# A tail tile's fifth channel block as three matmuls of 512 columns in place of six of 256

## The chip, the cores and the metric

The kernel runs on one core of one Trainium2 chip. The metric is the device time of one execution in microseconds, as the median of several runs. Engines are written as in the profile: PE for TensorE, PEld for its weight loads, DVE for VectorE, ACT for ScalarE, POOL for GpSimd, SP for SyncE, which issues most of the transfers.

## The reference, cut to what matters

The input `x` holds 2 x 4096 tokens of 640 channels in fp32. Two branches are mixed by a gate for each token: a spectral branch (a real Fourier transform over the tokens, a small block-wise network on the frequencies, and the transform back), and a gated feed-forward branch. The change lies in the second.

```python
def _B_ref(x, w_gate, w_up, w_down):
    return (_gelu(x @ w_gate) * (x @ w_up)) @ w_down      # 640 -> 1728 -> 640

x = A_x
g = _sigmoid((x * gate_w).sum(-1, keepdims=True))
a = _A_ref(x, A_w1, A_b1, A_w2, A_b2)                     # the spectral branch
b = _B_ref(x, B_w_gate, B_w_up, B_w_down)
return g * a + (1 - g) * b
```

## The kernel before

Every fp32 operand of a matmul is split into a high and a low part (`split`, lines 275 to 284: ACT copies the high part, DVE subtracts to get the low one), both kept in the type float32r. One product of two such operands is three matmuls: high by high, high by low, low by high. `prod` (line 461) writes out these three for each pair of operands, and `run` (line 470) issues the list into one part of a PSUM bank; `first` says whether the first matmul of the list starts a new sum or adds to what the bank holds.

The kernel has three stages in time. The gate and up products x @ w_gate and x @ w_up come first, up to about 1388 us, with the forward transform threaded in between (`a_step`, line 605); then the block-wise network on the frequencies; and from about 1812 us on the down product with the inverse transform. The order is written out by hand: no scheduler moves anything. `hook(k)` calls inside the products run small pieces of preparation that a table (`slots`) puts at chosen places.

In the first stage the tokens are taken in 16 blocks of 512, and the 1728 hidden columns in 14 tiles: tiles 0 to 12 have 128 gate columns and 128 up columns each, and the last, tile 13 (`NPAIR`), has the 64 gate columns and 64 up columns that remain, side by side in one weight tile of 128 columns. The tiles are dealt with in three groups (0 to 3, 4 to 7, 8 to 13); `keys` lists the pairs of group and token block, 48 in all. Tiles 0 to 12 go through `quad` (line 492), which forms the gate and up products by a scheme with seven block products of 6 or 9 matmuls each (`plain`, line 547, does the first ones directly). Tile 13 goes through `mixed` (line 564), once for each of the 16 keys of the third group, after the second `quad` of the key (line 1339). The page puts all matmuls of `run` on line 472, those of the spectral stages on line 295 (`mms`) and others.

The 640 channels are five slices of 128. Slices 0 to 3 lie in four operand tiles of 512 columns, `b11`, `b21`, `b12` and `b22`: `b11` and `b21` hold two channel slices each for the first 256 tokens of the block, `b12` and `b22` for the other 256. The fifth slice lies in `k4`, whose 512 columns are all 512 tokens of the block for that one slice. `x_of` (line 480) cuts these tiles into operands of 256 columns; `("k4", q)` asks for the q-th half of `k4`. Each is a pair of high and low. So `mixed` of before runs, for each half of the tokens, five channel slices of three matmuls each, all of 256 columns: 30 matmuls into one bank, 256 columns of it for each half.

Behind the products, `mixed` takes a gelu of the first 64 partitions (ACT, line 573), copies the other 64 (ACT, line 574), multiplies the two (DVE, line 575) and hands the result to the store `h_store`. A `memset` on POOL (line 572) clears the half of `h` that the tail tile does not fill.

Of the kernel before, what the change touches and what calls it, by code (L numbers as in the profile page):

```python
# [213 lines left out]
def spectral_mix_kernel(ctx: ExitStack, tc: tile.TileContext, a):  # L214
# [12 lines left out]
    def bank():  # L227
        return psum.tile([P, 512], F32, name="bank", tag="bank")
# [13 lines left out]
    def small(shape, dt=F32, name="small"):  # L242
        return pool.tile(shape, dt, name=name, tag="small", bufs=18)
# [217 lines left out]
    def prod(ws, x):  # L461

        ops = []
        for (wh, wl), (xh, xl) in zip(ws, x):
            ops += [(wh, xh), (wh, xl), (wl, xh)]
        return ops
# [3 lines left out]
    def run(dst, ops, first=True):  # L470
        for i, (l, r) in enumerate(ops):
            nc.tensor.matmul(dst, l, r, start=first and i == 0, stop=i == len(ops) - 1, skip_group_check=True)  # L472
            while inner and i == 1:
                inner.pop()()

    def h_store(tp, t, h):
        st(dr(hD, 4 * tp * P * 14 * P + t * P, [[14 * P, P], [P * 14 * P, 4], [1, P]]),
           h.rearrange("p (t n) -> p t n", t=4))

    def x_of(o, *names):  # L480

        tiles = []
        for n in names:
            n, q = n if isinstance(n, tuple) else (n, None)
            h, l = o[n]
            for k in ((0,) if n == "t5" else (0, 1) if q is None else (q,)):
                tiles.append((h[:, 256 * k:256 * k + 256], l[:, 256 * k:256 * k + 256]))
        return tiles
# [75 lines left out]
    def mixed(key):  # L564

        o, w = XO[key], WG[NPAIR]
        ws = [(w[:, k, 0], w[:, k, 1]) for k in range(5)]
        pm = bank()
        for q, (x0, x1) in enumerate((("b11", "b21"), ("b12", "b22"))):
            run(pm[:, 256 * q:256 * q + 256], prod(ws, x_of(o, x0, x1, ("k4", q))))  # L570
        s, h = small([P, 512], name="gelu"), small([P, 512], name="h")
        nc.gpsimd.memset(h[64:], 0.0)  # L572
        nc.scalar.activation(s[:64], pm[:64], AF.Gelu_apprx_tanh)
        nc.scalar.activation(h[:64], pm[64:], AF.Copy)
        nc.vector.tensor_mul(h[:64], s[:64], h[:64])
        h_store(key[1], NPAIR, h)
# [739 lines left out]
    for i, key in enumerate(keys):  # L1316
# [16 lines left out]
        for j, t in enumerate(quads):  # L1333
            def hook(k):
                for f in slots.get((i, 7 * j + k), ()):
                    f()
            (quad if i else plain)(key, t, hook)
            if gr == 2 and j == 1:
                mixed(key)
            if i % 16 == 15:  # L1340
                WG.pop(t)
            if 0 < i + 1 < last and j == nq - 1:
                x_raw(keys[i + 2])
            n = len(late)
            for f, *args in todo.get((i, j), []):
                f(*args)
            new = late[n:]
            del late[n:]
            flush()
            late.extend(new)  # L1350
# [126 lines left out]
```

## Time and profile before

| What | Value |
|---|---|
| Median of 3 runs | 2547.28 us |
| The three runs | 2546.24, 2550.69, 2547.28 us |
| Profiled execution | span 2546.4 us; the page lists no time of its own around it |
| Busy PE / DVE / ACT / POOL | 2535.1 / 2055.1 / 1502.8 / 370.2 us |
| Matmuls in all | 20276, of which 11736 of 256 columns from `xo` on line 472 |
| DMA | 483.48 MB, mean 190 GB/s |

The span runs from the first to the last instruction of one profiled execution. Busy times are unions: matmuls overlap, so that a PE that is busy throughout need not be at its peak, and the mean duration of one matmul in a group is its latency, not the distance to the next.

### The profile page before, as it was taken

How to read it: one execution, taken by the hardware profiler on the slowest of the kernel's cores; microseconds unless marked ns; L12 is line 12 of the kernel's file. 1: busy time of each engine (PE TensorE's matmuls, PEld its weight loads, DVE VectorE, ACT ScalarE, POOL GpSimd, SP SyncE). 2: the span in 40 equal slices, each digit the busy share in tenths (PEclk: the TensorE clock that was granted, in tenths of full speed). 3: DMA queues.
4: the chain of work that ended last, by engine and by line, in shares of the span. 5: the costliest groups of instructions: out<-in, count | busy, mean ns of one | idle time of the engine just before them, and what ended most of it. 6: DMA issues, size and time to landing. Idle time of an engine off the chain costs nothing.

```text
span 2546.4 us, 54296 instructions
## 1 busy us (share of the span) xinstructions
PE 2535.1 (100%) x20276; PEld 2530.4 (99%) x20276; DVE 2055.1 (81%) x4212; ACT 1502.8 (59%) x3490; POOL 370.2 (15%) x370
## 2 busy tenths in 40 slices
PE   9999999999999999999999999999999999999999
PEld 9999999999999999999999999999999999999999
DVE  7778777777777766776667788888899999999998
ACT  6555555666665655555556777778644444445443
POOL 0000000000000000000002111111133333333332
PEclk9999999999999999999999999999999999999999
DMA  6565657676767667776667455548844444344442
GB/s 232 190 215 196 212 170 234 205 236 211 219 205 249 207 213 231 224 230 214 212 222 223 129 153 150 160 137 266 291 149 138 150 156 158 120 144 156 155 136 92
DMA packets 346060, 483.48 MB, mean 190 GB/s; under 512 B 24701, under 2 KB 222717, under 8 KB 345797
## 3 DMA queue, kind: packets, MB, share of 16 engines
q1 hardware_dynamic: 331108, 438.47, 54.5%
q0 software_dynamic: 14688, 41.56, 4.5%
q8 instruction: 159, 2.61, 0.4%
q14 instruction: 105, 0.85, 0.1%
HBM read 300.29 MB, written 179.64 MB: 188 GB/s over the span
## 4 chain that ended last, share of the span: by engine, by line
PE 97%; DMA 1%; DVE 1%; issue 0%; ACT 0%; SPq 0%; DVEq 0%; ACTq 0%
PE bank L472 77%; PE bank L295 14%; PE bank L783 3%; PE bank L619 1%; DMA wx<-wdf 1%; PE bank L861 1%; PE bank L860 1%; DMA wx<-wdl 0%; PE bank L863 0%; DVE xo L279 0%; DMA wraw<-in_wgu_dram 0%; DVE xd L430 0%; DVE h L543 0%; DVE w L279 0%; DVE wl L715 0%
## 5 line engine op out<-in xcount | busy, mean ns | idle before, releaser
L472 PE MATMUL bank<-xo,w 128*128 128x256 f32 x11736 | 1362.0, 277 | 6.3 <-ACT xo L276 5.1
L472 PEld LDWEIGHTS bank<-xo,w 128*128 128x128 f32 x11736 | 1353.0, 188 | 7.5 <-ACT xo L276 5.1
L472 PE MATMUL bank<-wx,ho 128*128 128x320 f32 x4608 | 678.6, 308 | 0.1
L472 PEld LDWEIGHTS bank<-wx,ho 128*128 128x128 f32 x4608 | 674.1, 188 | 0.6 <-DMA wx<-wdf 0.3
L498 ACT ACTIVATE u<-bank 128x256 f32<-128x256 f32 x408 | 156.7, 384 | 258.0 <-PE bank L472 252.5
L279 DVE TENSOR_TENSOR ho<-hraw,ho 128x640 fp32r<-128x640 f32 (+3 forms) x384 | 276.9, 761 | 5.0 <-ACT ho L276 3.0
L276 ACT ACTIVATE ho<-hraw 128x640 fp32r<-128x640 f32 x320 | 166.3, 574 | 64.1 <-PE bank L472 46.8
L498 ACT ACTIVATE p<-bank 128x256 f32<-128x256 f32 x204 | 78.6, 385 | 149.0 <-PE bank L472 66.4
L279 DVE TENSOR_TENSOR xo<-xraw,xo 128x512 fp32r<-128x512 f32 x209 | 142.9, 684 | 25.2 <-ACT xo L276 24.7
L531 DVE TENSOR_TENSOR u<-bank,u 128x256 f32<-128x256 f32 x204 | 85.9, 421 | 90.8 <-ACT u L498 88.2
L279 DVE TENSOR_TENSOR xs<-xr,xs 64x640 fp32r<-64x640 f32 x128 | 105.0, 820 | 58.0 <-ACT xs L276 56.0
L1165 ACT ACTIVATE uu<-bank,gs 128x320 f32<-128x320 f32 x120 | 55.0, 525 | 160.0 <-PE bank L295 157.7
L295 PE MATMUL bank<-wm,h 128*128 128x320 f32 (+1 forms) x792 | 137.8, 309 | 0.0
L540 DVE TENSOR_TENSOR u<-bank,u 128x256 f32<-128x256 f32 x204 | 85.5, 419 | 62.2 <-PE bank L472 61.3
L276 ACT ACTIVATE xo<-xraw 128x512 fp32r<-128x512 f32 x209 | 131.0, 627 | 7.1 <-DMA xraw<-in_xT_dram 5.3
L621 DVE TENSOR_TENSOR as<-bank,as 64x320 f32<-64x320 f32 x256 | 113.9, 484 | 25.0 <-ACT as L620 24.0
L295 PEld LDWEIGHTS bank<-wm,h 128*128 128x128 f32 (+1 forms) x792 | 118.6, 185 | 1.2
L276 ACT ACTIVATE ho<-hs 128x640 fp32r<-128x640 f32 (+1 forms) x128 | 71.9, 576 | 77.8 <-PE bank L472 57.7
L572 POOL MEMSET h<- 64x512 f32 x16 | 8.4, 522 | 747.7 <-PE bank L619 369.4
L514 DVE TENSOR_TENSOR p<-bank,p 128x256 f32<-128x256 f32 x204 | 86.5, 424 | 36.6 <-PE bank L472 32.2
L279 DVE TENSOR_TENSOR s2s<-s,s2s 128x320 fp32r<-128x320 f32 x128 | 111.6, 929 | 0.9 <-ACT s2s L276 0.9
L620 ACT ACTIVATE as<-bank 64x320 f32<-64x320 f32 x256 | 96.8, 427 | 16.5 <-PE bank L619 14.0
(157 smaller groups left out, 3470.7 us busy)
## 6 DMA issues: line engine op xcount, KB each, us to landing
xo<-xD SPq DMA_DIRECT2D x124, 512.0 KB
xraw<-in_xT_dram SPq DMA_DIRECT2D x225, 256.0 KB
hD<-h SPq DMA_DIRECT2D x224, 256.0 KB
hraw<-hD SPq DMA_DIRECT2D x128, 320.0 KB
xD<-xo POOLq DMA_DIRECT2D x64, 512.0 KB, 4.4
sc<-scr SPq DMA_DIRECT2D x65, 320.0 KB
xr<-in_x_dram SPq DMA_DIRECT2D x64, 320.0 KB
scr<-as SPq DMA_DIRECT2D x64, 320.0 KB
```

The costliest lines, as they stand in the source:

```text
L276: nc.scalar.activation(dst, src, AF.Copy, scale=scale)
L279: eng.tensor_sub(dst, src, hi.bitcast(F32))
L295: nc.tensor.matmul(dst, l, r, start=i == 0, stop=i == len(ops) - 1)
L472: nc.tensor.matmul(dst, l, r, start=first and i == 0, stop=i == len(ops) - 1, skip_group_check=True)
L498: copy = lambda d, s_: nc.scalar.activation(d, s_, AF.Copy)
L514: nc.vector.tensor_add(p1, A, p1)
L531: nc.vector.tensor_add(u4, C, u4)
L540: nc.vector.tensor_add(u2, C, u2)
L620: nc.scalar.activation(stg[hi, cs], pa[lo, :320], AF.Copy)
L621: nc.vector.tensor_add(stg[hi, cs], pa[hi, :320], stg[hi, cs])
L783: nc.tensor.matmul(pz[:, kp * P:(kp + 1) * P], SC[b, c, kp][:, o:o + P], ft, start=True, stop=True)
L1165: nc.scalar.activation(uu[n2][:, cs], pe[:, :320], AF.Copy, scale=gs[:, b, 0, n2:n2 + 1])
```

## The change

In `mixed`, the fifth channel slice is taken out of the two loops over the token halves. Its three matmuls are run once over all 512 columns of `k4`, into the whole bank, and ahead of the others; they start the sum. The two loops then run four channel slices each and add to what the bank holds (`first=False`). The matmuls of a call go from 30 of 256 columns to 3 of 512 and 24 of 256. Nothing else is touched.

```diff
         pm = bank()
+        run(pm, prod(ws[4:], [o["k4"]]))
         for q, (x0, x1) in enumerate((("b11", "b21"), ("b12", "b22"))):
-            run(pm[:, 256 * q:256 * q + 256], prod(ws, x_of(o, x0, x1, ("k4", q))))
+            run(pm[:, 256 * q:256 * q + 256], prod(ws[:4], x_of(o, x0, x1)), first=False)
```

## The prediction

> **What bounds the kernel now.** The page comes first, its busy table, its clock row and its chain. TensorE (PE) works for practically the whole span, at the full granted clock, and the chain that ended last is PE work for 97% of it; 77% is line 472, the matmul inside `run`.
>
> ```profile
> span 2546.4 us, 54296 instructions
> ...
> PE 2535.1 (100%) x20276; PEld 2530.4 (99%) x20276; DVE 2055.1 (81%) x4212; ACT 1502.8 (59%) x3490; POOL 370.2 (15%) x370
> ...
> PEclk9999999999999999999999999999999999999999
> ...
> PE 97%; DMA 1%; DVE 1%; issue 0%; ACT 0%; SPq 0%; DVEq 0%; ACTq 0%
> PE bank L472 77%; PE bank L295 14%; PE bank L783 3%; PE bank L619 1%; DMA wx<-wdf 1%; PE bank L861 1%; PE bank L860 1%; DMA wx<-wdl 0%; PE bank L863 0%; DVE xo L279 0%; DMA wraw<-in_wgu_dram 0%; DVE xd L430 0%; DVE h L543 0%; DVE w L279 0%; DVE wl L715 0%
> ```
>
> The cores view gives the clock without rounding:
>
> ```profile
> core 0: 2546.4 us, clock 1.000
> ```
>
> The waits of PE, all of them, come to 6.6 us in six waits, of which one takes 5.1 us:
>
> ```profile
> PE bank L472 <- ACT xo L276: 5.1, 1, 5.1
> PE bank L472 <- ACT u L498: 0.9, 3, 0.5
> PE bank L472 <- DVE xo L279: 0.4, 1, 0.4
> PE bank L295 <- DVE ys L279: 0.2, 1, 0.2
> ```
>
> The edited function `mixed` is marked by its gelu on line 573: 16 of them, the first at 834.0 us and the last at 1363.1 us. The windows view for that stretch, with the stages before and behind it, shows PE busy without a gap in the edited stage and nearly without one after it.
>
> ```profile
> L573 ACT ACTIVATE gelu<-bank x16: 593/593/593, 834.0 to 1363.1; 64x512 f32<-64x512 f32 x16
> ```
>
> ```profile
> 50.00:834.00 784.00, 783.74 (x6833) 783.26 (x6833) 590.93 (x1333) 467.85 (x1119) 32.97 (x63) 1.00 0.67 214
> 834.00:1370.00 536.00, 536.00 (x4677) 536.00 (x4676) 369.29 (x849) 311.47 (x754) 20.12 (x34) 1.00 0.71 223
> 1370.00:1388.00 18.00, 17.30 (x146) 16.83 (x145) 14.29 (x29) 10.00 (x27) 8.55 (x10) 1.00 0.68 192
> 1388.00:1812.00 424.00, 423.73 (x3264) 421.26 (x3264) 351.25 (x772) 335.05 (x800) 51.44 (x37) 1.00 0.57 174
> ```
>
> The columns are the stretch, its length, the busy time of PE, weight load, DVE, ACT and POOL with instructions in brackets, and the clock, the DMA share and GB/s. So a nanosecond given to or taken from PE in `mixed` goes one for one into the end: no PE slack is there to swallow it, and in 1370 to 1812 PE has under 1 us idle in which later work could take it back.
>
> **What one matmul costs.** The durations in the group rows (277 ns for 256 columns) overlap, so the price is the distance from one start to the next. It is read from unbroken runs in the timeline: the run's length less one matmul's latency, over its count less one.
>
> ```profile
> L472 PE MATMUL bank<-xo,w 128*128 128x256 f32 x11736 | 1362.0, 277 | 6.3 <-ACT xo L276 5.1 <-ACT u L498 0.9 <-DVE xo L279 0.4
> L472 PE MATMUL bank<-wx,ho 128*128 128x320 f32 x4608 | 678.6, 308 | 0.1
> L783 PE MATMUL bank<-f,sc 128*128 128x128 f32 x640 | 82.1, 275 | 0.0
> ```
>
> ```profile
> 1004.18 19.68 PE L472 MATMUL bank<-xo,w 128*128 128x256 f32 x172
> ...
> 2017.81 21.19 PE L472 MATMUL bank<-wx,ho 128*128 128x320 f32 x144
> ...
> 1499.76 1.61 PE L783 MATMUL bank<-f,sc 128*128 128x128 f32 x13
> ```
>
> For 256 columns (19.68 - 0.277) / 171 = 113.5 ns; for 320 columns (21.19 - 0.308) / 143 = 146.0 ns; for 128 columns (1.61 - 0.275) / 12 = 111.3 ns. Two things are to be seen. Halving 256 columns saves 2 ns, so 128 columns stand on a floor of some 111 ns that is not columns, and 256 columns lie just above it. And 64 columns more than 256 cost 32.5 ns, so from there on the columns are paid. The floor does not add to the column time (else 128 and 256 would differ by more), so a matmul twice as wide cannot be expected to save one floor; it saves only what 256 columns cost above their own share.
>
> **The change, part by part.** Each call of `mixed` drops six matmuls of 256 columns (three products for each token block) and issues three of 512. The other 24 stay at 256 columns. Over 16 calls that is 96 out and 48 in, and 48 weight loads fewer. No other engine gets or loses an instruction. In the order in which the two programs stand, 30 matmuls in a row become 3 and then 24, at the same 16 places, none of them with a wait, and the instructions of the other engines keep their order.
>
> *Removed:* 96 x 113.5 ns = 10.90 us, all of it on the path.
>
> *Added:* 48 x T. No row shows a matmul of 512 columns, so T is bounded by the rows of 256 and 320. At the top stands the slope between them, 32.5 / 64 = 0.508 ns per column: 113.5 + 256 x 0.508 = 243.5 ns, in all 11.69 us, a loss of 0.79 us. At the bottom, 512 columns cannot take less than 320 do: 146.0 ns, 7.01 us, a gain of 3.89 us; that end asks for 192 columns free of charge, against the 32.5 ns that 64 were charged. Between them lie twice the 256 row, 227.0 ns (10.90 us, nothing either way), and the 320 row by proportion, 146.0 x 512 / 320 = 233.6 ns (11.21 us, +0.32 us). I take 233.6 ns, because the 320 row is the nearest in width and the only one clear of the floor. The sum is **+0.32 us** on PE.
>
> The Trainium skill, "TensorE: Matmul & The Clock Gate", section "Back-to-back issue gap", gives an isolated warm gap of N / 2.4 + 2.5 ns. That is 215.8 ns at 512 columns, and as an estimate by that page the sum would be 48 x 215.8 - 10,896 = -0.54 us. The trace does not follow it closely: the same formula says 109.2 and 135.8 ns for 256 and 320 columns, where the runs above gave 113.5 and 146.0.
>
> *Weight loads.* The 48 that go are hidden now: the weight-load row is busy beside the matmuls for the whole stretch (536.00 of 536.00 us). What they held up is inside the 113.5 ns, so they are not counted again. The cover of those that stay is a matmul of at least 256 columns, as before.
>
> *Moved ahead: the fifth channel tile.* Its operands `k4` and the fifth slice of the weight tile are now needed at the start of `mixed` instead of 12 matmuls later. Neither can be late: the products `g1` and `s3` of both quads ahead of `mixed` have read both halves of the same `k4`, and the weight tile is read whole by the former order, too, within 15 matmuls (1.7 us). So the move costs nothing. If that cover were missing, the wait would be at most those 12 matmuls, 1.36 us, once.
>
> *The bank.* The wide matmul opens the whole bank; formerly its second half was opened 15 matmuls later. Nothing reads the bank between, so no wait arises, and the readers come behind the last matmul as before:
>
> ```profile
> 830.83 3.79 PE L472 MATMUL bank<-xo,w 128*128 128x256 f32 x32
> ...
> 834.04 0.59 ACT L573 ACTIVATE gelu<-bank 64x512 f32<-64x512 f32 x1 [1.61 <-PE bank L472]
> ...
> 834.64 0.60 ACT L574 ACTIVATE h<-bank 64x512 f32<-64x512 f32 x1
> ...
> 835.27 0.39 ACT L498 ACTIVATE p<-bank 128x256 f32<-128x256 f32 x1
> ```
>
> ACT stands waiting when the last matmul ends (1.61 us here). Queued behind that wait are `h`, then the `p` copy of the next quad, which ends at 835.66. PE needs it only when it comes back to that bank: g1, half5, s3 and g2 of the next quad stand before, 33 matmuls or 3.7 us, thus at about 837.7. That leaves 2 us of slack against a shift of 20 ns per call, 3 x 233.6 - 6 x 113.5. Transfers hang on the same tail (the store of `h`) and move by as little.
>
> The profiled execution's span, 2546.4 us, is 0.9 us under the median of the three runs, 2547.28 (2546.24 to 2550.69). The span becomes 2546.7 us and the median 2547.28 + 0.32 = **2547.6 us**. A measurement of this kernel can tell about 0.2% from no change, 5.1 us; the sum is a sixteenth of that.
>
> **The rivals.**
>
> *A wide matmul at half rate: slower.* The one thing that no row shows is a 512-column matmul of this data type filling a whole bank. If its stream were served at half the rate of the 256 row, it would take 4 x 113.5 = 454 ns: 48 x (454 - 227) = +10.9 us, 2558.2 us, 0.43% slower. It decides from T = 333 ns on (5.1 us / 48 = 106 ns above 227). For it speaks only that the price per column rises from 0.443 ns (256) to 0.456 ns (320); against it, that this rise is 3%, where over 40% is needed.
>
> *Wide matmuls overlap further: faster, but barely to be seen.* If successive matmuls of that width were pipelined into one another, T would fall to the lower bound, the 146.0 ns of the 320 row: -3.9 us, 2543.4 us, 0.15% faster. Against it stands that the 144 matmuls in the 320 run do no such thing; they pay 32.5 ns for 64 columns. The Trainium skill, same page and section, says that in a stream of weight loads and matmuls a matmul of 512 columns sustains some 131 ns, less than its isolated gap. As an estimate by that page the change would bring 48 x 131 - 10,896 = -4.6 us. The trace speaks against it with 146.0 ns for fewer columns, and the page's 81 ns for 128 columns is 111.3 ns here.
>
> *The wide matmul is run as two halves, each with its weight load:* the change does not do what it says, and the time stays 2547.3 us.
>
> *A new wait in `mixed`*, the 1.36 us from above for late operands, in every call and not once: 16 x 1.36 = +21.8 us at most, 2569.4 us; it passes the 0.2% from 0.32 us per call on. Against it, the order of the instructions carries no wait at these places.
>
> **How the numbers follow.** Forecast 0.90; half rate 0.03; further overlap 0.03; two halves 0.02; new wait 0.02. Of the forecast I give 0.01 each to a median that strays beyond 0.2% by the spread of the runs, which is 4.5 us from lowest to highest. Faster by over 0.2%: 0.01 of that, and 0.01 of the overlap, whose 0.15% may be a little more: 0.02. Slower by over 0.2%: the 0.03 of half rate, 0.01 of the forecast and 0.01 of the wait (half of its cases are small): 0.05. Within 0.2%: the rest, 0.93. The range runs from the lowest run less 1.1 us (a wide matmul a tenth cheaper than two narrow ones, 48 x 22.7 ns), 2545.1 us, to the highest run plus the slope's 0.8 us, 2551.5 us. It leaves out the half rate, the overlap and the waits, together 0.08, and the strays.
>
> **What would show it right or wrong.** In the changed profile line 472 should list 48 matmuls of 512 columns and 11,640 of 256 from `xo`, and the distance between the first and the last gelu of `mixed`, 529.1 us now, should stay within 0.8 us. Timeline runs with three wide matmuls should be 20 ns longer each; a T under 227 ns would turn the sign of the sum but not its size. PE's waits should stay the four rows above. The prediction is wrong if the wide matmuls stand over 333 ns apart, if a wait for `xo` or `w` appears on PE at a call of `mixed`, or if PE's idle time grows in the stages behind 1370 us.

## The result and the profile after

The changed kernel takes 2564.81 us (median of 3 runs, 2563.88 to 2564.88) against 2547.28 us. It is slower, by 17.5 us on the medians, where 2547.6 us was forecast. On the means of the runs the ratio is 1.0065, with a 95% interval of 1.0042 to 1.0087. In the busy table and the chain of the page after, PE's work is longer and little else has changed; the clock stays at 1.000.

```profile
span 2563.1 us, 54200 instructions
...
PE 2550.9 (100%) x20228; PEld 2544.4 (99%) x20228; DVE 2062.1 (80%) x4212; ACT 1502.4 (59%) x3490; POOL 371.2 (14%) x370
...
PE 98%; DVE 1%; DMA 0%; ACT 0%; issue 0%; POOL 0%; DVEq 0%; ACTq 0%
```

PE does 48 matmuls fewer and is busy 15.8 us longer. The waits of PE add up to 0.9 us more than before. There are two new rows, of 0.9 and 0.2 us, and the first of them lies at the end of the stage, at 1397 us, not at a call of `mixed`:

```profile
PE bank L472 <- ACT xo L276: 5.1, 1, 5.1
PE bank L472 <- ACT p L498: 0.9, 1, 0.9
PE bank L472 <- ACT u L498: 0.8, 3, 0.5
PE bank L472 <- DVE xo L279: 0.3, 1, 0.3
PE bank L472 <- DVE ho L279: 0.2, 1, 0.2
PE bank L295 <- DVE ys L279: 0.2, 1, 0.2
```

The gelu of `mixed` (its line is now 574) is 544.1 us from first to last, 529.1 us before: 15.0 of the 16.7 us arise between the calls, 1.0 us in each interval. Another 1.0 us is there before the first call: it comes about in the first 123 us, where the two programs are the same. The windows view puts the stages beside one another; from 1405 us on nothing has changed (423.73 us of PE work for the same 3264 matmuls).

```profile
L574 ACT ACTIVATE gelu<-bank x16: 591/592/593, 835.2 to 1379.3; 64x512 f32<-64x512 f32 x16
```

```profile
835.00:1387.00 552.00, 552.00 (x4643) 550.07 (x4643) 371.25 (x850) 312.69 (x756) 21.72 (x35) 1.00 0.69 217
1387.00:1405.00 18.00, 16.42 (x138) 15.81 (x137) 14.19 (x28) 9.19 (x25) 7.90 (x9) 1.00 0.61 178
1405.00:1829.00 424.00, 423.73 (x3264) 421.25 (x3264) 351.46 (x772) 334.70 (x800) 51.48 (x37) 1.00 0.56 174
```

The groups by form show where: the 48 wide matmuls are cheap, and 11,640 untouched ones of 256 columns have 1369.6 us, where 11,736 had 1362.0. Their mean latency went from 277 to 279 ns.

```profile
L472 PE MATMUL bank<-xo,w 128*128 128x256 f32 x11640 | 1369.6, 279 | 7.2 <-ACT xo L276 5.1 <-ACT p L498 0.9 <-ACT u L498 0.8
L472 PE MATMUL bank<-xo,w 128*128 128x512 f32 x48 | 13.7, 393 | 0.0
```

The timeline of PE, one key long, shows it run by run. (A row takes neighbouring matmuls of one line together; the three wide ones are inside the row of 169.)

```profile
864.68 0.45 PE L620 MATMUL bank<-xs,f 128*128 128x320 f32 x2
864.97 20.30 PE L472 MATMUL bank<-xo,w 128*128 128x256 f32 x169
885.11 0.46 PE L620 MATMUL bank<-xs,f 128*128 128x320 f32 x2
885.41 1.46 PE L472 MATMUL bank<-xo,w 128*128 128x256 f32 x11
886.71 0.46 PE L620 MATMUL bank<-xs,f 128*128 128x320 f32 x2
887.00 9.11 PE L472 MATMUL bank<-xo,w 128*128 128x256 f32 x76
895.96 0.45 PE L620 MATMUL bank<-xs,f 128*128 128x320 f32 x2
896.24 5.00 PE L472 MATMUL bank<-xo,w 128*128 128x256 f32 x41
```

The run of 76 holds no edited instruction and takes 9.11 us, and the run of 41 takes 5.00. These are the same runs in the trace of before:

```profile
884.14 8.80 PE L472 MATMUL bank<-xo,w 128*128 128x256 f32 x76
...
893.07 4.83 PE L472 MATMUL bank<-xo,w 128*128 128x256 f32 x41
...
919.40 9.14 PE L472 MATMUL bank<-xo,w 128*128 128x256 f32 x76
```

8.80 became 9.11. The last row, still of before, is one to dwell on: a run of the same 76 matmuls in the next key, at the price of the changed kernel. The two prices were there from the start.

Taken one by one, the trace's records say what they are. Here are the start, the gap to the previous start, the modelled latency and the columns around a call in the changed kernel (all in ns):

```
  start    gap  latency  columns
 831193    113    276    256
 831306    113    276    256
 831420    114    388    512
 831646    226    398    512
 831881    235    393    512
 832112    231    281    256
 832231    119    280    256
 832348    117    281    256
 832466    118    281    256
 832583    117    281    256
```

Matmuls of 256 columns run in one of two steady patterns. In the quick one the gaps are 113 or 114 ns, 113.33 on average, and the latency is 276 or 277; in the slow one the gaps go 117, 118, 119 with a period of three, 117.78 on average, at a latency of 280 to 282, and each third weight load takes 192 ns where the others take 187 or 188. A pattern, once there, lasts through hundreds of matmuls. Counted by latency (279 to 282 ns for the slow pattern), line 472 has 1101 matmuls of 256 columns in it before and 4697 after; these are the counts called "slow" below. The 3596 more, at 117.78 - 113.33 = 4.45 ns each, are 16.0 us; 3444 of them, 15.3 us, lie between 826 and 1420 us, the stage of `mixed`. The wide ones occupy 231.1 ns on average up to the next start, 48 x 231.1 - 96 x 113.5 = +0.2 us. With the 0.9 us of waits that is 17.1 us, against 16.7 us of span.

### The profile page after: what moved, and what is told of

Same layout as the page of the kernel before. It is cut to its first block, busy times and chain, and to the rows that moved or that the text cites. A ratio compares the mean times of both kernels' runs of the same rounds, so it can differ in the third digit from the quotient of the medians.

```text
span 2563.1 us, 54200 instructions
## 1 busy us (share of the span) xinstructions
PE 2550.9 (100%) x20228; PEld 2544.4 (99%) x20228; DVE 2062.1 (80%) x4212; ACT 1502.4 (59%) x3490; POOL 371.2 (14%) x370
## 4 chain that ended last, share of the span: by engine, by line
PE 98%; DVE 1%; DMA 0%; ACT 0%; issue 0%; POOL 0%; DVEq 0%; ACTq 0%
PE bank L472 78%; PE bank L295 14%; PE bank L784 3%; PE bank L620 1%; PE bank L862 1%; PE bank L861 1%; PE bank L864 0%; DMA wx<-wdf 0%; DVE ho L279 0%; DVE xo L279 0%; DMA wraw<-in_wgu_dram 0%; DVE xd L430 0%; DVE w L279 0%; POOL hs L1117 0%; PE bank L798 0%
## 5 line engine op out<-in xcount | busy, mean ns | idle before, releaser
L472 PE MATMUL bank<-xo,w 128*128 128x256 f32 (+1 forms) x11688 | 1378.1, 279 | 7.2 <-ACT xo L276 5.1
L279 DVE TENSOR_TENSOR ho<-hraw,ho 128x640 fp32r<-128x640 f32 (+3 forms) x384 | 282.3, 776 | 4.5 <-ACT ho L276 2.5
```

The lines of the kernel that those rows point to most:

```text
L279: eng.tensor_sub(dst, src, hi.bitcast(F32))
```

## The experiments

The kernel before was timed again beside each batch: 2547.19 us (15 runs) beside the first four, 2547.98 (20 runs) beside the next four, 2547.96 (9 runs) beside the last three. The edits are shown against the changed kernel. My theory was that the wide matmuls set the slow pattern for those behind them; the first rival was that the new order did it.

**The order alone.**

```diff
-        run(pm, prod(ws[4:], [o["k4"]]))
+        for q in range(2):
+            run(pm[:, 256 * q:256 * q + 256], prod(ws[4:], x_of(o, ("k4", q))), first=not q)
```

> The fifth channel slice is run ahead of the others, as in the change, but as six matmuls of 256 columns (the second half of the bank joins the sum with first=False). Theory: the wide matmuls cost only 12 ns per call themselves, but leave PE in a slower steady pattern, 117.8 ns from start to start in place of 113.3 ns, for the 256-column matmuls behind them. Without wide matmuls the time is that of before, 2547 us within 2, with about 1100 of the 256-column matmuls of line 472 in the slow pattern as before. Rival: the order (the fifth slice first, the bank opened whole) does it: 2560 us or more, with about 4700 in the slow pattern.

2547.82 us, 1.0004 (0.9995 to 1.0013), 1038 slow. The order costs nothing; the width is what matters. The timeline rows are those of before:

```profile
859.03 4.83 PE L472 MATMUL bank<-xo,w 128*128 128x256 f32 x41
...
863.99 19.68 PE L472 MATMUL bank<-xo,w 128*128 128x256 f32 x172
...
885.36 8.80 PE L472 MATMUL bank<-xo,w 128*128 128x256 f32 x76
```

**The wide ones last.**

```diff
-        run(pm, prod(ws[4:], [o["k4"]]))
         for q, (x0, x1) in enumerate((("b11", "b21"), ("b12", "b22"))):
-            run(pm[:, 256 * q:256 * q + 256], prod(ws[:4], x_of(o, x0, x1)), first=False)
+            run(pm[:, 256 * q:256 * q + 256], prod(ws[:4], x_of(o, x0, x1)), first=not q)
+        run(pm, prod(ws[4:], [o["k4"]]), first=False)
```

> The three matmuls of 512 columns stand behind the 24 of 256. Theory: the slow pattern begins with the wide ones wherever they stand, so the 24 narrow ones of the call escape it: 16 x 24 x 4.5 ns = 1.7 us less than the changed kernel, about 2563 us, the slow stretch starting with the first matmul of the next quad. Rival (the order does it): 2547 us, no slow stretch.

2561.46 us, 1.0056 (1.0041 to 1.0071), 3805 slow. The slow stretch begins behind the wide ones, now with the next quad, as the theory has it. There are 892 slow matmuls fewer than in the changed kernel. Of these, 297 lie from 826 us on, where 384 were expected for the 24 that escape. The others lie ahead of the first call, where all the programs are the same; the count up to 700 us is 210 here and 799 in the changed kernel's profile, so it differs from one execution to the next.

**`mixed` a quad earlier.**

```diff
-            if gr == 2 and j == 1:
+            if gr == 2 and j == 0:
                 mixed(key)
```

> The changed mixed, called after the first quad of each key in place of the second. In the trace of the change the slow pattern ended at the second pair of transform matmuls (line 620) of each key, which lies in the second quad. Theory: that pair ends it again, so it lasts for 24 matmuls of mixed and some 29 of the second quad, 53 per call in place of 265: 16 x 53 x 4.5 ns = 3.8 us and 0.2 us for the wide ones, about 2551 us. Rival (the pattern lasts for a number of matmuls or a time, or to the same place of the schedule by chance): 2560 us or more.

2557.50 us, 1.0037 (1.0024 to 1.0050), 2873 slow: neither theory nor rival. The transform pair in the second quad did not end the pattern; it came back three matmuls behind the pair. But the trace holds the finding of the study. From 897 us on, in every other key, 7 in all, the slow pattern lasted until the next call, and there the three wide matmuls ended it:

```
  start us  matmuls             gaps ns
   896.02   9 of 256, slow      117
   897.08   3 of 512
   897.78   2 of 256            234, 121
   898.02   51 of 256, quick    113
```

So a wide matmul does not set the slow pattern; it seemed to change whichever pattern was there. In the changed kernel's own trace 14 calls leave the slow pattern behind, and the two that found it already there end it.

**A single wide one.**

```diff
-        run(pm, prod(ws[4:], [o["k4"]]))
+        run(pm, prod(ws[4:], [o["k4"]])[:1])
+        for q in range(2):
+            run(pm[:, 256 * q:256 * q + 256], prod(ws[4:], x_of(o, ("k4", q)))[1:], first=False)
```

> Only the first of the three products of the fifth slice is one matmul of 512 columns; the other two are four of 256. Theory: a single wide matmul is enough to change the pattern: 2562 to 2565 us, as the change. Rival (the wide ones have to follow one another, each making up part of it): 2547 to 2550 us, few matmuls in the slow pattern.

2557.38 us, 1.0036 (1.0022 to 1.0050), 3363 slow. One is enough: all 16 calls leave the slow pattern behind. It costs less than the expected 2562 since here the first transform pair behind the call ended the pattern, after 145 matmuls, in all 14 keys that have one.

**Two wide ones: the test of the toggle.**

```diff
-        run(pm, prod(ws[4:], [o["k4"]]))
+        run(pm, prod(ws[4:], [o["k4"]])[:2])
+        for q in range(2):
+            run(pm[:, 256 * q:256 * q + 256], prod(ws[4:], x_of(o, ("k4", q)))[2:], first=False)
```

> Two of the three products are wide, the third is two of 256. In the run with mixed after the first quad, the three wide ones ended the slow pattern where PE was in it already. If each wide matmul toggles the pattern, two leave it as it was: 2547 to 2549 us. If a wide one sets the slow pattern whatever was before, two act as one or three: 2557 to 2565 us, slow from the second one on.

2548.28 us, 1.0001 (0.9992 to 1.0010), 918 slow. Two cancel: 15 calls leave PE quick as they found it, and the last one, which found it slow, left it slow. By the groups it has 32 wide matmuls, twice the 16 of the run before, and the mean latency is back at 277:

```profile
L472 PE MATMUL bank<-xo,w 128*128 128x256 f32 x11672 | 1356.8, 277 | 6.4 <-ACT xo L276 5.1 <-ACT u L498 0.8 <-DVE xo L279 0.3
L472 PE MATMUL bank<-xo,w 128*128 128x512 f32 x32 | 10.0, 393 | 0.0
```

**Three, apart from one another.**

```diff
-        run(pm, prod(ws[4:], [o["k4"]]))
-        for q, (x0, x1) in enumerate((("b11", "b21"), ("b12", "b22"))):
-            run(pm[:, 256 * q:256 * q + 256], prod(ws[:4], x_of(o, x0, x1)), first=False)
+        k = prod(ws[4:], [o["k4"]])
+        n = [(q, m) for q, x in ((0, x_of(o, "b11", "b21")), (1, x_of(o, "b12", "b22"))) for m in prod(ws[:4], x)]
+        for i in range(3):
+            run(pm, k[i:i + 1], first=not i)
+            for q, m in n[8 * i:8 * i + 8]:
+                run(pm[:, 256 * q:256 * q + 256], [m], first=False)
```

> The three wide matmuls stand apart, each with eight of 256 columns behind it. If each toggles the pattern: slow, quick, slow in the three stretches of eight, and slow behind the call as after one wide matmul, about 2557 us. If a wide one always sets the slow pattern: slow in all three and 2557 to 2565 us.

2557.19 us, 1.0038 (1.0025 to 1.0051), 2986 slow. The toggle can be seen at work, in all 16 calls alike:

```
  start us  matmuls             gaps ns
   862.83   22 of 256, quick    113
   865.33   1 of 512
   865.55   8 of 256, slow      226, then 117 to 118
   866.50   1 of 512
   866.73   2 of 256            233, 122
   866.97   6 of 256, quick     114
   867.65   1 of 512
   867.87   125 of 256, slow    226, then 118
```

**The same columns, 320 wide.**

```diff
-        run(pm, prod(ws[4:], [o["k4"]]))
+        for c in (slice(0, 192), slice(192, 512)):
+            run(pm[:, c], prod(ws[4:], [(o["k4"][0][:, c], o["k4"][1][:, c])]), first=not c.start)
```

> The fifth slice ahead as three matmuls of 192 and three of 320 columns, the same columns as three of 512, the 320 directly ahead of the narrow ones. Theory: it is the width that turns the pattern, far above 320 columns; the transform's pairs of 320 never did it where PE was in the quicker pattern (113.3 ns), so PE stays quick: 2547 to 2549 us, about 1100 in the slow pattern. Rival: any matmul clearly longer than its weight load, several in a row, does it: 2557 us or more.

2559.72 us, 1.0047 (1.0032 to 1.0062), 3492 slow: the theory fell here, and the rival held. No matmul of a call is wider than 320, and all 16 calls leave the slow pattern behind. The transform's matmuls of 320 come in pairs, and a pair mostly leaves the quick pattern as it is, as two wide ones do. If that is the reason, one of 320 by itself should turn the pattern.

**One of 320.**

```diff
-        run(pm, prod(ws[4:], [o["k4"]]))
+        for q in range(2):
+            run(pm[:, 256 * q:256 * q + 256], prod(ws[4:], x_of(o, ("k4", q)))[:2], first=not q)
+        wl, kh = ws[4][1], o["k4"][0]
+        for c in (slice(0, 192), slice(192, 512)):
+            run(pm[:, c], [(wl, kh[:, c])], first=False)
```

> The fifth slice ahead of the others; two of its products are narrow, the third is one matmul of 192 and then one of 320 columns. Theory: what counts is whether the number of matmuls longer than 256 columns between narrow ones is odd; a pair of 320 leaves the quick pattern as it is, one alone turns it: slow behind it, 2556 to 2560 us. Rival: 320 columns alone are too few to turn it, only three in a row added up to it: 2547 to 2549 us.

2557.19 us, 1.0037 (1.0024 to 1.0050), 2866 slow; all 16 calls leave the slow pattern behind. A short matmul of 192 columns and one of 320 cost some 9 us beside two of 256. Which of the two turns the pattern is not shown: in this run and in the one before, matmuls of 192 stand directly ahead of those of 320, and short matmuls can turn it too, as the next run and the last section show. The rows hold the same number of matmuls as in the run with the order alone, 172, and take 0.65 us more:

```profile
861.62 20.33 PE L472 MATMUL bank<-xo,w 128*128 128x256 f32 x172
```

**A short one behind the wide.**

```diff
         run(pm, prod(ws[4:], [o["k4"]]))
+        wh, xh = ws[0][0], o["b11"][0]
+        for c in (slice(0, 128), slice(128, 256)):
+            run(pm[:, c], [(wh, xh[:, c])], first=False)
+        run(pm[:, :256], prod(ws[:4], x_of(o, "b11", "b21"))[1:], first=False)
+        run(pm[:, 256:], prod(ws[:4], x_of(o, "b12", "b22")), first=False)
```

> The change, but the first narrow product behind the three wide matmuls is two of 128 columns in place of one of 256. Theory: a wide matmul leaves weight loading and streaming in another phase, and a stream that is much shorter than its load brings them back: PE is quick again within a few matmuls; 16 more matmuls at some 110 ns cost 1.8 us, the wide ones 0.2 us: about 2549 us. Rival: the pattern ends only where a matmul waits for another engine (the transform pairs wait for the split operands); two short ones change nothing: 2564 us or more.

2549.04 us, 1.0009 (0.9999 to 1.0018), 777 slow. In the 15 calls that found PE quick, the 256-column matmuls behind the two short ones are quick again after five that are not. The last call found PE in the slow pattern, and there the stream went on slow, at 117 to 119 ns. So the short ones do not restore the quick pattern as such: three wide and two short together leave whichever pattern was there, as two wide ones do. The time is 1.1 us above that of before, less than the 2 us expected, and the interval holds no difference at all.

**When a transform pair ends the slow pattern.** With the period of three in mind, the number of slow matmuls up to the pair was changed by moving the wide ones by one or two places.

```diff
-        run(pm, prod(ws[4:], [o["k4"]]))
-        for q, (x0, x1) in enumerate((("b11", "b21"), ("b12", "b22"))):
-            run(pm[:, 256 * q:256 * q + 256], prod(ws[:4], x_of(o, x0, x1)), first=False)
+        a = prod(ws[:4], x_of(o, "b11", "b21"))
+        run(pm[:, :256], a[:2])                       # a[:1] in the second run
+        run(pm, prod(ws[4:], [o["k4"]]), first=False)
+        run(pm[:, :256], a[2:], first=False)          # a[1:]
+        run(pm[:, 256:], prod(ws[:4], x_of(o, "b12", "b22")), first=False)
```

> The change with two of the 24 narrow matmuls ahead of the three wide ones. In the slow pattern three matmuls form a period (gaps of 117, 118 and 119 ns, weight loads of 187, 188 and 192 ns), and whether the next transform pair ends it went by the number of narrow matmuls since the wide ones, modulo three: 141 and 117 (rest 0) stayed, 53 and 125 (rest 2) came back after three matmuls, 145 (rest 1) was ended. Theory: with 139 in between (rest 1) the first pair ends it in every call: some 139 slow matmuls per call in place of 224, 16 x 139 x 4.45 ns = 9.9 us, 2557 us. Rival: the number does not matter, the wide triple decides: as the change, 2563 us or more.

> The change with one of the 24 narrow matmuls ahead of the wide ones: 140 up to the first pair, rest 2. Theory: as in the two runs with rest 2 of which the next pair lies 13 matmuls on, the slow pattern comes back behind the first pair (distance 143 ns within the pair) and is ended by the second (149 ns): some 150 per call, 2558 us. Rival: as the change, 2563 us or more.

Two ahead: 2557.01 us, 1.0036 (1.0022 to 1.0051), 2729 slow; the first pair ended the pattern in all 14 keys that have one. One ahead: 2558.60 us, 1.0040 (1.0025 to 1.0055), 2932 slow; the first pair (142 to 144 ns from start to start) let it come back, the second, 13 matmuls on, ended it (148 to 150 ns), again in all 14. The timeline of the first of the two shows the end of it: 169 matmuls, of which the last 139 are in the slow pattern and the three wide ones stand ahead of these, and the 11 behind the pair at the quick price of 1.42 us, where the changed kernel had 1.46.

```profile
861.35 20.31 PE L472 MATMUL bank<-xo,w 128*128 128x256 f32 x169
881.49 0.45 PE L622 MATMUL bank<-xs,f 128*128 128x320 f32 x2
881.78 1.42 PE L472 MATMUL bank<-xo,w 128*128 128x256 f32 x11
```

In the changed kernel the first pair stands at 141, the number that leaves the pattern on (151 to 152 ns), and in 13 of the 14 keys it is the fourth pair that ends it. That is why three wide ones cost 17 us there and 9 us two places later.

The count since the wide matmuls holds only behind matmuls of 512 columns: in the two runs with 320, a pair at 141 let the pattern come back. What holds in all 13 traces is the place of the pair behind the last weight load of 192 ns. If that is the load just ahead of the pair's own, the pattern comes back (111 pairs, 142 to 145 ns from start to start); if it is one place further ahead, the pattern stays (90 pairs, 151 to 152 ns); two places further, it ends (133 pairs, 148 to 150 ns). That covers each of the 334 pairs that stand in a steady slow stretch, without an exception.

Over all these runs the time follows the count, within 2 us. With 4.45 ns for each slow matmul above the 1101 of before, the spans should differ from 2546.4 us by +16.0 (the change; 16.7 measured), +12.0 (wide last; 12.6), +10.1 (one wide; 9.7), +8.4 (three apart; 9.0), +7.2 (two ahead; 6.8), +7.9 (one of 320; 8.1), +10.6 (192 and 320; 10.6), +7.9 (a quad earlier; 9.8), +8.1 (one ahead; 9.7), -0.8 (two wide; -0.1) and -0.3 us (order alone; +0.9). For the short ones behind the wide the count gives -1.4 us, and 16 more matmuls at some 111 ns add 1.8; 0.6 us was measured. The furthest off is the quad earlier, by 1.9 us.

## Why the prediction was wrong

*The price of the wide matmul* was right: 231.1 ns, where 233.6 was taken. In the 14 calls that found PE quick, the first of the three takes 225 or 226 ns, which is two quick narrow ones (2 x 113.3), the second 235 or 236 ns, which is two slow ones (2 x 117.8), and the third 230 or 231. The bounds held, and neither half rate nor further overlap showed. The Trainium skill, "TensorE: Matmul & The Clock Gate", section "Back-to-back issue gap", lies below the measured 231.1 ns with both its figures for 512 columns: an estimate of 215.8 ns by its formula for the isolated gap, and some 131 ns sustained.

*The step that failed* is the sentence "The other 24 stay at 256 columns", with the weight loads "as before": it took the price of an untouched matmul for a constant. The sum was made over the 144 matmuls that the edit takes out or puts in; the time went into 3596 others, most of them in the quads, which the diff doesn't name. Each of these costs 4.45 ns more, 16.0 us in all. The 113.5 ns had been read from one unbroken run at 1004 us; the row of 9.14 us for 76 matmuls stands 85 us ahead of it in the same trace.

*That a nanosecond on PE goes one for one into the end* was right: what PE had gained in length by the end of the stage, 16.9 us, is 16.7 us at the end of the span. *The operands, the bank and the readers behind it* were right: no wait arose at a call, and the order alone cost nothing.

*The rivals.* The time that came, 2564.8 us, was inside what "slower" was given (0.05), but by none of its mechanisms: no wait, and no half rate. The range was built from the price of 48 matmuls and the spread of the runs, so it could not hold it.

*The check that the prediction itself named*, three wide matmuls 20 ns longer than six narrow ones and a distance between the gelus within 0.8 us, is what gave it away: the first came out at 12 ns, the second at 15.0 us. PE's idle time behind 1370 us, another of its signs, did grow, but by 0.9 us only.

## What to carry to other kernels

Where PE is the bound and issues a matmul of the same shape thousands of times, an edit is not priced by its own instructions alone: after every change read the gap of the untouched matmuls, run by run, before and behind the edit. In this kernel wide matmuls among narrow ones did no harm where two stood together, or three with two of 128 columns behind them; one or three cost 9 to 17 us over 16 places. If a timeline shows one run of the same length at two durations, that is a price list with two entries, and the question is what chooses between them.

## What the hardware showed that was not expected

PE streams 256 float32r columns, each matmul with its own weight load, in two patterns that go on by themselves, with starts 113.3 or 117.8 ns apart, at the same granted clock of 1.000 and without a wait. A single matmul of 512 columns in the stream changes the pattern, in either direction; the next one changes it back. One of 192 and one of 320 together change it, too. A pair of 320 in the slow pattern ends it or does not, and which of the two goes by the matmul of the three-matmul period at which the pair stands; the outcome was predicted for two kernels and came out in all 14 keys of each.

Wide matmuls are not needed for it. The kernel before changes its pattern at a group of eight matmuls of 128 columns, which belong to the forward transform:

```profile
1339.81 12.40 PE L472 MATMUL bank<-xo,w 128*128 128x256 f32 x108
1352.05 1.05 PE L783 MATMUL bank<-f,sc 128*128 128x128 f32 x8
1352.85 22.86 PE L472 MATMUL bank<-xo,w 128*128 128x256 f32 x192
```

Ahead of the group the gaps are 113.3 ns, behind it 117.8; the next such group, at 1375.55 us, turns the stream back. The first two of these groups change the pattern in each of the 13 traces, 26 times in all: 9 times from quick to slow, 17 times from slow to quick. The slow pattern also sets in elsewhere in the kernel before, which has 1101 of its matmuls in it, for example from 920.2 us on, behind a matmul that started 78 ns after its weight load began in place of 110 and was followed by a gap of 149 ns.

What it is that alternates in PE stays open. In both patterns the next weight load starts 2 to 5 ns behind the start of a matmul; the matmul follows its own load by 110 ns in the quick one and by 114 to 115 in the slow one. The Trainium skill, same page, section "Step-by-step: what each phase is for", says that PE pulls a weight load ahead of running matmuls when the row groups do not conflict or when the load goes to a background buffer. That fits loads which run beside the matmuls, but no run here shows the buffers, and nothing was tried that would tell a buffer in turn from, say, two clocks out of step. No version was found that beats the kernel before: a wide matmul takes what two narrow ones take, so that there was nothing to win even with the pattern kept.
